# A fused attention, Mish layer and soft mixture of experts: expert weights multiplied in even-odd pairs, first expert layer handed over in halves, and a new task order

## The chip, the cores and the metric

One NeuronCore of a Trainium2 chip runs the program. Its engines are TensorE (PE: matmuls, and PEld: the weight loads that precede them), VectorE (DVE), ScalarE (ACT), GpSimd (POOL) and SyncE (SP), whose queue issues all the DMAs here. Each engine works through its own instructions in order. The metric is the device time of one execution in microseconds.

## The reference

```python
# attention, for 2 batches x 8 heads, 768 positions, 64 wide
k_sum = k.reshape(B, H, nb, 32, D).max(axis=3); v_sum = v.reshape(B, H, nb, 32, D).mean(axis=3)
scores = concat([where(|i - j| < 16, scale * q @ k.T, -1e9), scale * q @ k_sum.T + log(32)])
attn = softmax(scores) @ concat([v, v_sum])        # x: 1536 tokens x 512
h = x @ w_in                                       # 512 -> 2048
g = h * tanh(softplus(h)); x = g @ w_out           # Mish; 2048 -> 512
logits = x @ phi                                   # 8 experts x 4 slots = 32 columns
d = softmax(logits, axis=0); slot_input = d.T @ x  # 32 slot vectors of 512
slot_out[e] = relu(slot_input[e] @ w1[e]) @ w2[e]  # e = 0..7, 512 -> 1024 -> 512
out = softmax(logits, axis=1) @ slot_out
```

The layer w_out is never applied to the tokens: phi is multiplied into w_out once (W2), the logits are g @ W2, and the slot inputs are (d.T @ g) @ w_out.

## The kernel before

The 1536 tokens are 12 tiles of 128. The program first makes a list of tasks (`add`), and then emits them in the sequence of a table of task numbers, `ORDER`; a second table, `CHOICE`, says which engine takes a task that two could take. PSUM banks and SBUF slots are drawn from rings (`Ring`, `Hold`) as the tasks are emitted. So the tables fix the order on every engine, and the hardware only waits where data or a buffer is missing. In the rows below, `slot` is an SBUF slot of 8 KB for each partition and `bank` a PSUM bank; three banks (bank_61 to bank_63 in the order rows) hold the hidden layer's results.

For each tile t:

- Scores, L384 (mask) and L389; the row maximum on DVE (L400), negated on POOL or DVE (L404); exponentials on ACT (L414); normalised (L425, L426, L430); transposed on PE (L436); multiplied with the values (L446). The result goes to float16 as a high part on ACT (L451) and a low part on DVE (L452): that is x of the tile, and what the hidden layer waits for.
- Hidden layer: four blocks `fb` of 512 columns, each 12 float16 matmuls (L601, L602, L603, four times), into one bank, which ACT empties with the Mish function (L609).
- Routing: the Mish output g is split and transposed by DMA (tiles 0 to 9; L625, L627, L630) or transposed on PE (tiles 10 and 11, L642), multiplied with W2 into logits (L682, L685), summed over the four column groups (L700), turned into exponentials (L720), transposed (L734, L735), and multiplied with g (L757) into a running sum P_acc.

Ahead of that the weights w_in arrive as 64-bit words that ACT and DVE decode (L465, L467, L468), scale (L496, L289 to L297) and split (L502 high, L504 low); w_out the same way (L465 to L468, then L557 to L562 for W2, and L578 turns it). ACT has to load another function table (ACT_TABLE_LOAD) when it goes from exponentials or decodes to Mish or back.

The tail, after the last tile: P_acc is transposed (L881), multiplied with w_out (L890), scaled on DVE (L894), spread to the slot layout (L899, L905). Expert layer 1 (L921) is 64 matmuls with 32 weight columns each, so that one takes a quarter of TensorE's columns, a column group: expert e uses groups 0 and 1 when e is even, 2 and 3 when it is odd, and all go into one bank.

```python
    for k in range(16):
        e_, i = divmod(k, 2)
                    g = 2 * (e_ % 2) + half
                    pe.matmul(banks[hh.slot][32 * g:32 * g + 32], siM[:, 2 * i + c, 32 * e_:32 * e_ + 32], w[:, c, 512 * half:512 * half + 512], start=(e_ < 2 and i == 0 and c == 0), stop=(e_ >= E - 2 and i == 1 and c == 1), tile_position=(0, 32 * g))
```

Then relu (L926), transposes (L928), four copies into the layout for layer 2 (L934), and layer 2 (L975) in two stages: 384 output columns (weights w2a), then 128 (w2b). Each stage is multiplied with the token softmax, which three groups of transposes (L954) and copies (L955 to L957) prepare: L980 to L982 and L993 for the first stage, L995 for the second; L1003 and L1005 scale the results, L1007 stores them. L661 is a matmul whose result nobody reads, issued while PE would idle (18 times). The expert weights, 33.5 MB, come through L859 into slots as these come free.

Of the kernel before, what the change touches and what calls it, by code (L numbers as in the profile page):

```python
# [92 lines left out]
]  # L95
CHOICE = {
    "ACT": [
# [30 lines left out]
class Plan:  # L128
# [4 lines left out]
    def __init__(self):  # L133
        self.tasks = []
# [948 lines left out]
```

## Time and profile before

| | |
|---|---|
| device time, median of 3 runs | 315.11 us (314.45 to 315.95) |
| span of the profiled execution, first to last instruction | 314.3 us |
| busy: PE, ACT, DVE, POOL | 277.4, 202.7, 199.0, 41.5 us |
| granted TensorE clock, mean | 0.997 |
| DMA | 83.71 MB, 266 GB/s over the span |

The profiled execution's own time is its span with what lies before its first and behind its last instruction; only the span is in the profile, and the median is 0.8 us above it. Busy times of PE count matmuls that overlap as one. The granted clock is a share of 2.4 GHz.

### The profile page before, as it was taken

The numbers are of one execution on the slowest core, as the hardware profiler recorded it, in microseconds if no ns is written. First come the engines' busy times: TensorE is split into PE (matmuls) and PEld (weight loads), VectorE is DVE, ScalarE is ACT, GpSimd is POOL, SyncE is SP. The second block draws the span as 40 slices with busy tenths as digits, with TensorE's granted clock in tenths as the row PEclk, the third lists the DMA queues.
The fourth block names the chain that finished last, engine by engine and source line by source line (L and its number), as shares of the span: only waits on it lengthen the run. The fifth ranks groups of instructions, "written<-read, shape, count | busy, mean of one in ns | idle before, by whom it ended". The sixth has DMA issues, their size and how long they took to land.

```text
span 314.3 us, 7472 instructions
## 1 busy us (share of the span) xinstructions
PE 277.4 (88%) x2991; PEld 150.1 (48%) x2991; DVE 199.0 (63%) x454; ACT 202.7 (64%) x480; POOL 41.5 (13%) x54
## 2 busy tenths in 40 slices
PE   0336568789999999999999999999999999999992
PEld 0223435446555554646545445454455664334472
DVE  2589989989875877866696885774414544101271
ACT  1369889699856957887987597929647671002153
POOL 0020426403110122411101100100000010100000
PEclk9999999999999999999999999999999999999998
DMA  7999988996967487599269977898988998999948
GB/s 254 350 398 405 360 305 295 279 347 234 273 218 201 143 182 163 132 330 261 37 99 301 200 108 202 210 272 205 152 330 322 332 393 299 378 424 423 418 143 272
DMA packets 60435, 83.71 MB, mean 266 GB/s; under 512 B 44529, under 2 KB 48113, under 8 KB 56049
## 3 DMA queue, kind: packets, MB, share of 16 engines
q1 hardware_dynamic: 60400, 83.24, 85.9%
q8 instruction: 23, 0.38, 0.5%
q14 instruction: 12, 0.09, 0.1%
HBM read 69.60 MB, written 3.15 MB: 231 GB/s over the span
## 4 chain that ended last, share of the span: by engine, by line
PE 76%; DVE 9%; DMA 7%; ACT 3%; issue 3%; SPq 1%; POOL 1%; ACTq 0%; POOLq 0%; DVEq 0%
PE bank L601 13%; PE bank L602 12%; PE bank L603 12%; PE bank L921 5%; PE bank L975 5%; PE bank L757 4%; PE bank L389 4%; PE bank L446 3%; PE bank L436 3%; DMA slot<-wo 3%; PE bank L682 2%; PE bank L578 2%; DMA mask_sb<-masks 2%; DVE slot L468 2%; DMA slot<-kb 2%
## 5 line engine op out<-in xcount | busy, mean ns | idle before, releaser
L601 PE MATMUL bank<-slot,slot 128*128 128x512 f16 x192 | 73.4, 382 | 1.2 <-ACT slot L609 1.2
L602 PE MATMUL bank<-slot,slot 128*128 128x512 f16 x192 | 73.0, 380 | 0.0
L603 PE MATMUL bank<-slot,slot 128*128 128x512 f16 x192 | 72.8, 379 | 0.0
L609 ACT ACTIVATE slot<-bank,scal 128x512 f32<-128x512 f32 x48 | 32.3, 686 | 12.1 <-PE bank L603 11.6
L430 POOL TENSOR_TENSOR slot<-slot,sm 128x480 f32<-128x480 f32 x18 | 21.2, 1179 | 119.7 <-DVE sm L426 75.7
L630 DVE SCALAR_TENSOR_TENSOR slot<-slot,sc,slot 128x512 f16<-128x512 f32 x40 | 31.3, 789 | 2.4 <-ACT slot L625 2.0
L603 PEld LDWEIGHTS <-slot 128*128 128x128 f16 x192 | 18.8, 98 | 22.8 <-issue 0.3
L601 PEld LDWEIGHTS <-slot 128*128 128x128 f16 x192 | 18.8, 98 | 22.2 <-issue 5.5
L465 ACT ACTIVATE slot<-slot 128x1024 f32<-128x1024 f32 (+1 forms) x22 | 19.2, 897 | 14.4 <-DMA slot<-wi 10.7
L602 PEld LDWEIGHTS <-slot 128*128 128x128 f16 x192 | 18.8, 98 | 16.2 <-issue 1.4
L414 ACT ACTIVATE slot<-bank,sm 128x120 f32<-128x120 f32 x64 | 22.1, 363 | 3.7 <-POOL sm L404 3.7
L609 ACT ACT_TABLE_LOAD x18 | 23.1, 1283 | 0.3
L468 DVE SCALAR_TENSOR_TENSOR slot<-slot,slot 128x1024 int32<-128x1024 int32 (+1 forms) x22 | 22.5, 1025 | 0.6
L436 PE MATMUL bank<-ident_sb,slot 128*120 128x128 f32 x96 | 15.8, 289 | 6.4 <-POOL slot L430 5.5
L263 DVE COPY slot<-bank 120x512 f32<-120x512 f32 (+2 forms) x26 | 16.4, 638 | 6.0 <-PE bank L578 3.5
L261 ACT COPY slot<-bank 128x512 f32<-128x512 f32 (+1 forms) x23 | 13.1, 585 | 9.7 <-PE bank L436 5.0
L436 PEld LDWEIGHTS bank<-ident_sb,slot 128*120 128x120 f32 x96 | 11.6, 143 | 11.1 <-POOL slot L430 6.7
L627 DVE TENSOR_SCALAR slot<-slot,sc 128x512 f16<-128x512 f32 x31 | 15.7, 529 | 1.6 <-DMA slot<-slot 1.6
L446 PE MATMUL bank<-slot,slot 120*64 120x64 f32 x384 | 14.8, 233 | 1.7 <-DMA slot<-vh 1.7
L921 PE MATMUL bank<-slot,slot 128*32 128x512 f32 x128 | 15.9, 595 | 0.0
L446 PEld LDWEIGHTS bank<-slot,slot 120*64 120x64 f32 x384 | 13.1, 145 | 5.7 <-issue 2.1
L975 PE MATMUL bank<-slot,slot 128*32 128x384 f32 (+1 forms) x256 | 15.5, 381 | 0.0
(154 smaller groups left out, 460.1 us busy)
## 6 DMA issues: line engine op xcount, KB each, us to landing
slot<-w SPq DMA_DIRECT2D x16, 1024.0 KB, 7.4
slot<-w2a SPq DMA_DIRECT2D x12, 960.0 KB, 7.2
slot<-wo SPq DMA_DIRECT2D x8, 1024.0 KB, 7.4
slot<-wi SPq DMA_DIRECT2D x6, 1024.0 KB, 8.2
slot<-kh SPq DMA_DIRECT2D x12, 384.0 KB, 6.5
slot<-vh SPq DMA_DIRECT2D x12, 384.0 KB, 7.4
slot<-w2b SPq DMA_DIRECT2D x4, 1024.0 KB, 17.9
slot<-kb SPq DMA_DIRECT2D x4, 768.0 KB, 5.9
```

Source lines behind the costliest of these rows:

```text
L414: sca.activation(A_b[ha.slot][:, hp], src, AF.Exp, bias=m[:, hp:hp + 1], scale=1.0 if late else 0.125, accum_out=m[:, 4 + hp:5 + hp])
L430: (pool if e == "POOL" else vec).tensor_tensor(A_b[ha.slot], A_b[ha.slot], sm_t[hq.slot][:, 4:8].unsqueeze(2).to_broadcast([128, 4, KW]), ...
L436: pe.transpose(banks[ht.slot][0:KW, 128 * hp:128 * hp + 128], A_b[ha.slot][:, hp], ident_sb)
L446: pe.matmul(banks[hm.slot][64 * r:64 * r + 64, 128 * hp + 64 * w:128 * hp + 64 * w + 64], Vb[i][:, w, c:c + 64], AT_b[hat2[r].slot][0:KW, ...
L468: d = add("DVE", dve(n), lambda e: vec.scalar_tensor_tensor(di(), st(0), 29, di(), op0=ALU.logical_shift_right, op1=ALU.bitwise_or), [d], ...
L601: pe.matmul(ps, x[:, 0, dc], w[:, 0, dc], start=(dc == 0), stop=False)
L602: pe.matmul(ps, x[:, 0, dc], w[:, 1, dc], start=False, stop=False)
L603: pe.matmul(ps, x[:, 1, dc], w[:, 0, dc], start=False, stop=(dc == 3))
L609: d = add("ACT", act(512) + 93, lambda e, fb=fb, hb=hb, sc=sc: sca.activation(slots[gd.slot][:, 512 * fb:512 * fb + 512], banks[hb.slot], ...
L630: d = add("DVE", dve(512) + 66, lambda e: vec.scalar_tensor_tensor(pv(1), g(), sfb[:, t // TB:t // TB + 1], pv(0), op0=ALU.mult, op1=ALU.s ...
L921: pe.matmul(banks[hh.slot][32 * g:32 * g + 32], siM[:, 2 * i + c, 32 * e_:32 * e_ + 32], w[:, c, 512 * half:512 * half + 512], start=(e_ < ...
L975: pe.matmul(banks[hh.slot][32 * j:32 * j + 32, 0:nc_], hM(fc // 4)[:, j, 32 * e_:32 * e_ + 32], w[:, o:o + nc_], start=(e_ == 0 and fc < 4 ...
```

## The change

Expert layer 1 is done by pairs of experts, even and odd: of each weight half the even expert's two matmuls (groups 0 and 1) are followed at once by the odd one's (groups 2 and 3). Experts 0 to 3 go into one bank and 4 to 7 into a second, and relu, transposes and copies are done once for each. The scaling L894 and the spreading L899 and L905 are cut into two halves of the columns; layer 1 needs only the first half to begin, and layer 2 only the first four experts.

All tables are new: `ORDER`, `CHOICE` and a third one, `SLOT`, that names each buffer (ring sizes and buffers are the same). Nothing else of the arithmetic differs; the weights w1 are loaded in the order of the pairs.

```diff
-        d = add("PE", 980, l1, [d, ex_ready[k]], p + 1, acq=[hh] if k == 0 else [], use=[ex_h[k]] + ([hh] if k else []))
...
-    d = add("ACT", act(512), lambda e, hh=hh: sca.activation(hs_t, banks[hh.slot], AF.Relu), [d], p + 1, use=[hh])
...
+    for u in range(2):
+        hh, ht2 = Hold(hring), Hold(tring)
+        for pr in range(2 * u, 2 * u + 2):
+            for i in range(2):
+                def l1(e, pr=pr, i=i, hh=hh):
+                    for c in range(2):
+                        for par in range(2):
+                            w = slots[ex_h[4 * pr + 2 * i + par].slot].rearrange("p (c f) -> p c f", c=2)
+                            for half in range(2):
+                                g, e_ = 2 * par + half, 2 * pr + par
+                                pe.matmul(banks[hh.slot][32 * g:32 * g + 32], siM[:, 2 * i + c, 32 * e_:32 * e_ + 32], w[:, c, 512 * half:512 * half + 512], start=(pr % 2 == 0 and i == 0 and c == 0), stop=(pr % 2 == 1 and i == 1 and c == 1), tile_position=(0, 32 * g))
...
-            src, n = w1[k // 2, k % 2].rearrange("p c f -> p (c f)"), 2048
...
+            kind, src, n = "ld_w1", w1[2 * (k // 4) + k % 2, k // 2 % 2].rearrange("p c f -> p (c f)"), 2048
...
 ORDER = [
-    7, 11, 8, 13, 23, 29, 2, 33, 21, 34, 35, 210, 3, 36, 211, 213, 30, 31, 214, 215, 32, 37, 38, 0, 41, 42, 43, 45,
```

What the tables do to the engines is shown in three places. The first is the start, where two engines move: SP's queue, before: its rows from the load of w_in's second block (`wi`, into slot_82) to that of the first tile's values (`vh`).

```order
L476 DMA slot_82<-wi 128x2048
L270 DMA bmean_sb<-bmean 128x144
L476 DMA slot_80<-wi 128x2048
L313 DMA slot_79<-vn 128x1536
L368 DMA slot_89<-qh 128x512
L369 DMA slot_90<-kh 128x768
L476 DMA slot_81<-wi 128x2048
L476 DMA slot_82<-wi 128x2048
L368 DMA slot_88<-qh 128x512
L370 DMA slot_88<-vh 96x1024
```

The same stretch of the queue of the changed kernel:

```order
L420 DMA slot_82<-wi 128x2048
L248 DMA bmean_sb<-bmean 128x144
L285 DMA slot_79<-vn 128x1536
L420 DMA slot_80<-wi 128x2048
L328 DMA slot_89<-qh 128x512
L329 DMA slot_90<-kh 128x768
L420 DMA slot_81<-wi 128x2048
L330 DMA slot_88<-vh 96x1024
```

The values of the first tile now stand ahead of one block of w_in (1024 KB) and one `qh` (256 KB). On ACT the rows between the x of tile 1 (the high part, L451) and the first Mish (L609), before; L414 are exponentials, L465 decodes, L502 the high part of w_in.

```order
L502 ACTIVATE slot_75<-slot_83,sm_113 128x1024
L414 ACTIVATE slot_91,sm_106<-bank_65,sm_106 128x120 x4
L414 ACTIVATE slot_91,sm_108<-bank_64,sm_108 128x120 x4
L465 ACTIVATE slot_76<-slot_80 128x1024
L451 ACTIVATE slot_92<-bank_68,scal 128x512
L465 ACTIVATE slot_77<-slot_81 128x1024
L465 ACTIVATE slot_77<-slot_82 128x1024
L609 ACT_TABLE_LOAD
L609 ACTIVATE slot_85<-bank_61,scal 128x512
L502 ACTIVATE slot_74<-slot_84,sm_107 128x1024
L609 ACTIVATE slot_85<-bank_62,scal 128x512
```

After, where the same operations are L403 (x), L529 (Mish), L368, L411 and L443:

```order
L443 ACTIVATE slot_75<-slot_83,sm_107 128x1024 x2
L403 ACTIVATE slot_92<-bank_67,scal 128x512
L240 COPY slot_91<-bank_66 120x512
L411 ACTIVATE slot_76<-slot_81 128x1024
L411 ACTIVATE slot_84<-slot_82 128x1024
L368 ACTIVATE slot_91,sm_108<-bank_64,sm_108 128x120 x4
L529 ACT_TABLE_LOAD
L529 ACTIVATE slot_85<-bank_63,scal 128x512
L529 ACTIVATE slot_85<-bank_61,scal 128x512
L529 ACTIVATE slot_85<-bank_62,scal 128x512
L403 ACTIVATE slot_92<-bank_68,scal 128x512
```

The first Mish now stands behind one decode of w_out (slot_76) instead of four (slot_76 and slot_77), and the x of tile 2 right behind three of them. The second engine is PE, in mid-program, around the multiplication of tile 3's exponentials with g (L757, bank_68; L436 is a transpose of another tile's attention weights, L601 to L603 are the hidden layer), before.

```order
L601 MATMUL bank_63<-slot_73,slot_92 128x512
L602 LDWEIGHTS slot_92
L602 MATMUL bank_63<-slot_73,slot_92 128x512
L603 LDWEIGHTS slot_92
L603 MATMUL bank_63<-slot_73,slot_92 128x512
L436 MATMUL bank_64<-ident_sb,slot_91 120x128 x4
L757 MATMUL bank_68<-slot_83,en_119 32x512 x4
L601 LDWEIGHTS slot_92
```

The same multiplication after (L651), with the scores L346, the values L399 and the logits L581:

```order
L633 MATMUL bank_68<-ident_sb,lp 128x32
L346 MATMUL bank_64<-slot_90,slot_88 64x120 x2
L346 MATMUL bank_65<-slot_90,slot_88 64x120 x2
...
L651 MATMUL bank_68<-slot_83,en_119 32x512 x4
L399 MATMUL bank_67<-slot_91,slot_88 64x64 x16
L581 LDWEIGHTS slot_88
L581 MATMUL bank_62<-slot_94,slot_88 32x128
```

Groups of matmuls that use a part of TensorE's rows or columns (scores, values, logits, L757) stand next to each other now. Over the whole program, PE goes 36 times from such a group to a full-array matmul, 61 times before; into a hidden-layer matmul 10 times, 33 before; into a transpose 15 times, 20 before; into another one, such as the sum L700, 11 times, 8 before. The third place is PE at expert layer 1, its first experts before (each row is four matmuls on column groups 0 and 1 or, from slot_82 on, on 2 and 3).

```order
L661 MATMUL bank_62<-mask_sb,spread_sb 128x480
L921 MATMUL bank_63<-slot_80,slot_94 32x512 x4
L921 MATMUL bank_63<-slot_81,slot_94 32x512 x4
L921 MATMUL bank_63<-slot_82,slot_94 32x512 x4
L921 MATMUL bank_63<-slot_90,slot_94 32x512 x4
L921 MATMUL bank_63<-slot_83,slot_94 32x512 x4
```

After, its first rows and its end (L781 spreads, L811 transposes for layer 2, L836 transposes for the softmax, L855 is layer 2):

```order
L781 MATMUL bank_68<-rep_sb,vsum 128x32 x2
L803 MATMUL bank_61<-slot_80,slot_94 32x512 x2
L803 MATMUL bank_61<-slot_81,slot_94 32x512 x2
...
L803 MATMUL bank_62<-slot_85,slot_94 32x512 x2
L803 MATMUL bank_62<-slot_92,slot_94 32x512 x2
L811 MATMUL bank_66<-ident_sb,vsum 128x128 x4
L836 MATMUL bank_61<-ident_sb,P_acc 128x128 x4
L811 MATMUL bank_65<-ident_sb,gx_t 128x128 x4
L855 MATMUL bank_62<-slot_95,slot_94 32x384 x4
```

Now every two matmuls are followed by two on the other column groups, and the two groups of transposes stand behind all 128, with one of the softmax's between them. The matmuls L661 that stood between the spreading and the first weights are gone. Of the three groups of transposes for the softmax (L954, now L836) one stands ahead of layer 2 in both kernels; the second stood in the middle of the first stage of layer 2 and the third at its end, and now both stand behind it.

## Rows read from the trace of the kernel before

**Rows 1.** Busy tenths of PE in 40 slices of the span.

```profile
PE   0336568789999999999999999999999999999992
```

**Rows 2.** Windows: span, busy PE, PEld, DVE, ACT, POOL, clock, DMA share, GB/s.

```profile
0.00:45.19 45.19, 18.24 (x200) 12.26 (x200) 33.73 (x68) 28.66 (x70) 8.87 (x18) 1.00 0.98 357
45.19:63.92 18.73, 15.00 (x156) 8.44 (x153) 18.28 (x35) 15.11 (x32) 9.37 (x9) 1.00 0.88 263
63.92:261.58 197.66, 197.10 (x2148) 107.21 (x2147) 134.34 (x319) 149.40 (x359) 22.22 (x26) 1.00 0.84 227
261.58:314.30 52.72, 47.04 (x492) 22.20 (x492) 12.64 (x35) 9.53 (x23) 1.06 (x1) 0.98 0.87 338
```

**Rows 3.** Timeline of PE, start: start, duration, operation, wait before and its releaser.

```profile
36.03 1.98 PE L446 MATMUL bank<-slot,slot 120*64 120x64 f32 x32 [1.68 <-DMA slot<-vh]
...
45.19 0.61 PE L601 MATMUL bank<-slot,slot 128*128 128x512 f16 x1
...
63.92 0.38 PE L601 MATMUL bank<-slot,slot 128*128 128x512 f16 x1 [1.22 <-ACT slot L609]
```

**Rows 4.** One window of the start, columns as in the second group.

```profile
20.00:40.00 20.00, 10.75 (x124) 7.52 (x124) 18.65 (x35) 17.60 (x33) 3.73 (x4) 1.00 1.02 385
```

**Rows 5.** Timeline of DVE: low parts of x for tiles 0, 1, 2.

```profile
41.23 0.74 DVE L452 SCALAR_TENSOR_TENSOR slot<-bank,scal,slot 128x512 f16<-128x512 f32 x1
...
59.87 0.74 DVE L452 SCALAR_TENSOR_TENSOR slot<-bank,scal,slot 128x512 f16<-128x512 f32 x1
...
72.61 0.74 DVE L452 SCALAR_TENSOR_TENSOR slot<-bank,scal,slot 128x512 f16<-128x512 f32 x1
```

**Rows 6.** Timeline of ACT ahead of the first Mish.

```profile
60.69 1.19 ACT L465 ACTIVATE slot<-slot 128x1024 f32<-128x1024 f32 x1 [2.88 <-DMA slot<-wo]
61.89 1.28 ACT L609 ACT_TABLE_LOAD   x1
```

**Rows 7.** Chain of work that ended last, 170 to 198 us: start, duration, what.

```profile
170.63 0.22 PE bank L700 x2
...
173.23 0.32 PE bank L601
173.55 0.21 PE bank L602
...
174.63 0.44 PE bank L436 x4
...
195.42 0.58 PE bank L436 x4
...
197.00 0.42 PE bank L700 x2
```

**Rows 8.** Timeline of PE in the tail.

```profile
261.58 3.64 PE L890 MATMUL bank<-slot,W 128*32 128x512 f32 x32 [0.35 <-ACT W L261]
...
267.71 15.90 PE L921 MATMUL bank<-slot,slot 128*32 128x512 f32 x128
...
285.94 5.35 PE L975 MATMUL bank<-slot,slot 128*32 128x384 f32 x60
291.22 0.66 PE L954 MATMUL bank<-ident_sb,P_acc 128*128 128x128 f32 x4
291.81 6.00 PE L975 MATMUL bank<-slot,slot 128*32 128x384 f32 x68
...
300.76 0.96 PE L993 MATMUL bank<-s_split,c_split 96*128 96x384 f32 x4
```

**Rows 9.** Timeline of ACT and of DVE between the expert layers.

```profile
283.66 0.60 ACT L926 ACTIVATE vsum<-bank 128x512 f32<-128x512 f32 x1 [21.85 <-PE bank L921]
...
285.20 0.62 DVE L934 COPY slot<-bank 128x64 f32<-128x64 f32 x4 [16.82 <-PE bank L928]
```

**Rows 10.** Windows from the last hidden matmul on, columns as before.

```profile
249.60:298.60 49.00, 48.58 (x442) 21.80 (x440) 11.57 (x38) 11.56 (x26) 2.12 (x2) 1.00 0.98 390
266.00:298.00 32.00, 32.00 (x289) 12.42 (x289) 3.39 (x15) 2.73 (x5) 1.06 (x1) 1.00 1.01 411
```

More of the change, by code (lines that the diff above doesn't have):

```diff
@@ L121 @@
 class Hold:
     def __init__(self, ring):
-        self.ring, self.users, self.end, self.slot, self.home = ring, 0, 0.0, None, ring
+        self.ring, self.home, self.users, self.slot, self.n = ring, ring, 0, None, None
 class Plan:
-    LAT = PR['lat']
     def __init__(self):
-        self.tasks = []
-    def add(self, eng, dur, fn, deps=(), prio=0.0, acq=(), use=(), lat=0.0):
-        t = dict(cost=eng if isinstance(eng, dict) else {eng: dur}, fn=fn, deps=[d for d in deps if d is not None], prio=prio, acq=list(acq), use=list(acq) + list(use), end=None, lat=lat, tab=0)
+        self.tasks, self.holds = [], []
@@ L138, in add @@
+    def add(self, engines, name, fn, deps=(), acq=(), use=(), tab=0, give=None, after=()):
+        t = dict(engines=engines.split(), name=name, fn=fn, deps=[d for d in deps if d is not None], after=[d for d in after if d is not None], acq=list(acq), use=list(acq) + list(use), tab=tab, give=give, done=False)
         for h in t["use"]:
             h.users += 1
+            if h.n is None:
+                h.n = len(self.holds)
+                self.holds.append(h)
         self.tasks.append(t)
@@ L143, in run @@
     def run(self):
-        clock, table = {}, 0
-        engine = {n: e for e, ns in CHOICE.items() for n in ns}
+        choice = {n: e for e, ns in CHOICE.items() for n in ns}
         for n in ORDER:
             t = self.tasks[n]
-            e = engine.get(n) or next(iter(t["cost"]))
-            start = clock.get(e, 0.0)
-            for d in t["deps"]:
-                same = d["eng"] == e and e not in ("DMA", "none")
-                start = max(start, d["end"] + (0.0 if same else self.LAT + d["lat"]))
+            assert all(d["done"] for d in t["deps"] + t["after"])
             for h in t["acq"]:
                 if h.slot is None:
-                    free = min(h.ring.free)
-                    h.ring.free.remove(free)
-                    h.slot = free[1]
-                    start = max(start, free[0] + self.LAT)
-            t["fn"](e)
-            t["eng"], t["end"] = e, start + t["cost"][e] + (1400.0 if t["tab"] and table and t["tab"] != table else 0.0)
-            table = t["tab"] or table
-            if e != "none":
-                clock[e] = t["end"]
+                    h.slot = SLOT[h.n]
+                    h.ring.free.remove(h.slot)
+            t["fn"](choice.get(n) or t["engines"][0])
+            t["done"] = True
+            if t["give"]:
+                t["give"][0].free.update(t["give"][1])
             for h in t["use"]:
                 h.users -= 1
-                h.end = max(h.end, t["end"])
                 if h.users == 0:
-                    h.home.free.append((h.end, h.slot))
-def act(n, psum=True, ptr=0):
-    return 0.83 * n + 160 if psum else 0.7 * n + 340 + 90 * ptr
-def dve(n, fast=False, psum=False):
-    return (0.52 if fast else 1.04) * n + 70 + 55 * psum
-def dma_ns(kib):
-    return kib * 1024 * 128 / (390.0 if kib > 6.5 else 345.0)
+                    h.home.free.add(h.slot)
+        assert len(ORDER) == len(self.tasks)
 @with_exitstack
@@ L650, in g_transpose, with tr @@
-        gT_h[t, fb] = h, done
-    chain = [None]
-    pacc = [None]
-    ssum_done = [None]
+        (g,) = g_done[t, fb]
+        def tr(e):
+            for j in range(4):
+                pe.transpose(banks[ht.slot][:, 128 * j:128 * j + 128], slots[g_h[t].slot][:, 512 * fb + 128 * j:512 * fb + 128 * j + 128], ident_sb)
+        q = add("PE", ("GT", t, fb), tr, [g], acq=[ht, h], use=[g_h[t]], after=gp_hi[-1:] + [last_G[0]])
+        last_G[0] = q
+        gT_h[t, fb] = h, [add("ACT DVE", ("GTc", t, fb), lambda e: copy_on(e, gT_b[h.slot].rearrange("p a k -> p (a k)"), banks[ht.slot]), [q], use=[ht, h])]
@@ L657, in local_summary_attention_mish_soft_moe, with busy @@
+    chain, pacc, ssum_done = [None], [None], [None]
     hw = Hold(hring)
-    def busy(after, n):
-        for _ in range(n):
-            add("PE", 200, lambda e: pe.matmul(banks[hw.slot][:, 0:480].rearrange("p (a k) -> p a k", a=4), spread_sb, mask_sb[:, 0].unsqueeze(1).to_broadcast([128, 4, KW]), start=True, stop=True), [after], -50.0, acq=[hw])
+    def busy(after, n, where):
+        for j in range(n):
+            add("PE", ("busy", where, j), lambda e: pe.matmul(banks[hw.slot][:, 0:480].rearrange("p (a k) -> p a k", a=4), spread_sb, mask_sb[:, 0].unsqueeze(1).to_broadcast([128, 4, KW]), start=True, stop=True), [after], acq=[hw])
@@ L855, in local_summary_attention_mish_soft_moe @@
             n = 384 * min(5, 64 - c)
[L856 removed]
+            kind, src = "ld_w2a" if n == 1920 else "ld_w2z", w2a[:, 384 * c:384 * c + n]
         else:
[L858 to L860 removed]
+            kind, src, n = "ld_w2b", w2b[k - 29].rearrange("p e c f -> p (e c f)"), 2048
+        ex_l.append(add("DMA", (kind, k), lambda e, h=h, src=src, n=n: dma(out=slots[h.slot][:, 0:n], in_=src), acq=[h], after=ex_l[-1:]))
         ex_h.append(h)
[L862 to L867 removed]
+    ex_ready = ex_l
     siM = part(22, 0, 1152).rearrange("p (c s) -> p c s", c=4)
@@ L908, in local_summary_attention_mish_soft_moe @@
     hx = Hold(expring)
     hM = lambda half: part(hx.slot, 0, 1152).rearrange("p (c s) -> p c s", c=4) if half else siM
[L910 removed]
+    hs_b = [hs_t, gx_t]
+    d = None
+    h_ok = []
     ex_done = {}
[L912 to L925 removed]
```

479 lines of the change are left out of this document (195 added, 284 removed), and 145 rows, old and new, of tables (CHOICE, ORDER, SLOT).

## The prediction

> **What bounds the kernel now.** I read the busy tenths first [rows 1]: PE is near full from about the eighth of forty slices to the last but one, and empty only at the start. Cutting the span into four stretches [rows 2] makes this exact. Up to 45.19 us, where the hidden layer begins on PE, PE is busy 18.24 us; up to 63.92, where the first Mish lets it go on [rows 3], 15.00 of 18.73. The idle time of both is 26.95 + 3.73 = 30.68 us. From 63.92 to 261.58 PE is busy 197.10 of 197.66 us, while DVE has 134.34 and ACT 149.40: PE bounds this stretch, and time can be saved there only by issuing PE's work earlier or by making it cheaper. The tail of 52.72 us is PE again (47.04), and DMA at 338 GB/s beside it. The granted clock is 1.00 in the first three stretches and 0.98 in the last, so I let it alone. The kernel is therefore the start, plus a fixed amount of PE work, plus the tail, and I price the change in these three.
>
> **Start (-7 us).** What holds PE here is in the rows. The values of tile 0 made PE wait 1.68 us, until 36.03 [rows 3]. The low half of x ends at 41.97, 60.61 and 73.35 for tiles 0, 1 and 2 (start plus 0.74) [rows 5], and the hidden layer of a tile can't begin before that. On ACT the first Mish is behind a decode that waited 2.88 us for w_out, to 60.69, took 1.19, and is followed by a table load of 1.28 [rows 6].
>
> After, the load of the values passes one block of w_in and one qh, 1024 + 256 KB or 1.31 MB; at the 385 GB/s of 20 to 40 us [rows 4] they land 3.4 us sooner, so the values matmul starts near 32.6. Its 1.98 us, then the x halves, put x of tile 0 ready near 38.3, and the first hidden matmul near 38.5 instead of 45.19, also because the scores of the next tile no longer stand ahead of the hidden matmuls behind a wait for a bank. I estimate x of tile 1 near 55.5 (5 us sooner) and of tile 2 near 62 (11 sooner), since three decodes of w_out move behind it on ACT and the values behind fewer loads. The first Mish has one decode ahead instead of four, which frees it of the wait of 2.88; I put it near 56 and PE's going on near 58.
>
> What this is worth: at 64.4 us the changed PE has 72 hidden matmuls behind it (the blocks fb 0 to 3 of tile 0 and some of tile 1 by the order), the old one 36 at 63.92. A hidden matmul behind another costs 0.21 to 0.22 us (the second of a run of them [rows 7]), so 36 are 7.8 us. Scores (1.5) and values (1.1) of the next tiles are done sooner too, less the 0.5 by which 64.4 is later: about 9.8 us. Against this speaks that the engines feeding PE have no slack here: from 20 to 40 us DVE is busy 18.65 and ACT 17.60 of 20 us [rows 4], and DVE 18.28 of 18.73 up to 63.92 [rows 2]. What is done sooner has to be done with engines 90 to 97% full. I take 7, nearer the upper bound since nothing of the work is added, and keep 0 (the idle time only moves to another wait) and 10 as ends.
>
> **Middle (-2.2 us).** PE's work is the same in number and shape, but the order groups the matmuls that use a part of the array. The first full-array matmul after such a group takes longer: 0.32 us (after the values) where the next one takes 0.21 [rows 7]. Transposes take 0.58 instead of 0.44 for four, and the sum L700 0.42 instead of 0.22 for two [rows 7]. By the order, hidden matmuls stand behind such a group 23 times less, transposes 5 times less, sums and others 3 times more: 23 x 0.11 + 5 x 0.14 - 3 x 0.20 = 2.6; I take 2.2, as the records' ends are modelled. Bounds are 0, if the longer row hides in the pipeline, and 2.6.
>
> All other edits of the tables I cost at nothing, because PE's 99.7% leaves no room in which DVE or ACT work shows. Eleven more of the float16 splits go from DVE to ACT (at 134 and 149 of 197 us neither is full), three normalisations from POOL, six table loads less on ACT (1.28 each [rows 6], 7.7 us of ACT time, not on the path). The cover is PE's queue of ready hidden blocks; if it runs dry, the third rival applies.
>
> **Tail (-3.2 us).** The parts are these.
> - Layer 1 took 15.90 us for 128 matmuls [rows 8]. L890 has matmuls of the same shape over all four groups: 32 in 3.64 us. That is eight steps of four at 0.43 us and 0.2 besides, so 128 over all groups are 32 x 0.43 + 0.2 = 13.9 (-1.9). Before, PE got to nearly this rate in the middle of the run, as it can start the next expert's groups while the others are still busy, and lost it at both ends. Bounds: 0 (it is order alone) and -2.1.
> - From the last of L890 (265.22 by its duration) to the first weights of layer 1 at 267.71 are 2.49 us [rows 8], with scaling, 8 small matmuls and a copy in series. In halves of the columns only the first half of each is ahead: 1.5 (-1.0).
> - From the end of layer 1 (283.61) to layer 2 at 285.94 are 2.33 us [rows 8]: relu 0.60 and four copies 0.62 [rows 9], with transposes between. After, the transposes of the second half wait for its relu, but its copies are needed only by expert 4: 0.60 + 0.44 and 0.2 of hand-over, 1.25 (-1.1).
> - One group of transposes leaves the middle of the first stage, 0.59 (291.22 to 291.81) [rows 8] (-0.6).
> - Two chains of the softmax now stand behind that stage instead of one. From its end (291.81 + 6.00) to the first L993 at 300.76 are 2.95 us [rows 8]; I put the new gap at 3.8 (+0.9). And 56 instead of 40 matmuls of the second stage remain at 128 columns after the first of them (+0.5).
> The sum is -3.2; bounds -5, if the two last parts are nothing, and +1, if the first three are.
>
> **Sum.** 314.3 - 7 - 2.2 - 3.2 = 301.9 us of span. The profiled execution's span is 0.8 us below the median of the runs, 315.11, so I forecast 302.7 us.
>
> **Rivals.**
> *1. The start's idle time only moves.* ACT and DVE are in order and nearly full, so an early x of tile 0 may be paid by a late one of tile 3. For it: the windows above. Against it: two of the waits are for DMAs whose loads really move. Only middle and tail would remain: 314.3 - 5.4 + 0.8 = 309.7 us.
> *2. The weights' DMA bounds the tail.* The last hidden matmul ends where the first of two windows begins, at 249.6 [rows 10]. Eighteen weight loads were left then by the queue's issues; about 21 are in the changed order, 1 MB each or 21.4 MB, because layer 1's slots come free later. PE would need the last of them some 54 us after that matmul (15.5 of work up to L890, 3.6, 1.5, 13.9, 1.3, 11.3, then about 7). At 411 GB/s, the rate of 266 to 298 [rows 10], they take 52 us: 2 us to spare. At 390, the mean of 49 us, 55: one late. At 357, the rate of the first stretch [rows 2], 60: 6 us late, which eats more than the gain of the tail, and gives 302.7 + 6 = 308.7. The Trainium skill ("DMA: Bandwidth & Descriptors", Where 436 GB/s comes from) says of transfers between HBM and SBUF that "the HBM side (~358) binds"; by it this rival, at its 308.7, would be the case. The trace speaks against it, with 411 GB/s over 32 us of the same loads.
> *3. A new stall in the middle: slower.* PE is in order, and a block of column-group matmuls now stands together ahead of hidden matmuls that are ready. If the data of the block (exponentials from ACT, transposed by DMA) is late by more than 1 us in each of the 12 tiles, the order loses 12.4 us and the gain is gone. For it: three hidden banks leave PE only three blocks of 12 matmuls, 7.8 us, of work to go on with. Against it: between the same tasks I count about as much PE work in the new order as in the old; only two places are tight (0.65 and 1.03 us). At 1.3 us a tile the time is 318.
> *4. The pairs don't do what they say*: PE already overlaps, and layer 1 stays at 15.8: 304.6, inside the range.
>
> **How the numbers follow.** The forecast or rival 4: 0.64, with 297 to 306.5 as its own range (start -10 to -4, middle and tail by their bounds). Rival 1: 0.16. Rival 2: 0.08. Rival 3: 0.08 over 316, and 0.04 that a weaker stall ends between. The range 297 to 311 leaves out rival 3 and a little at either end. A difference of 0.5% (1.6 us) is about what measurement of this kernel can tell from none, so faster means below 313.5: 0.64 + 0.16 + 0.08 = 0.88, less 0.02 for tails; same 0.06; slower 0.08.
>
> **What would show it.** Right: the first hidden matmul near 38.5 us without a wait for vh; PE going on after the first Mish before 60; PE idle for under 1 us from there to the expert layers; layer 1 in about 14 us; the gaps at both sides of layer 1 near 1.5 and 1.25 us; no wait for a weight. Wrong: a row of the hidden layer or of the scores in the middle with waits adding to more than 3 us; x of tile 1 or 2 as late as before; layer 2's second stage waiting for w2b; layer 1 above 15.5.

## The result and the profile after

The changed kernel takes 303.95 us (median of 4 runs, 302.84 to 304.82), the kernel before 314.78 in the same set: ratio 0.9652, 95% interval 0.9614 to 0.969, faster by 10.8 us. The profiled execution's span is 303.0 us, 11.3 below that of before. Its busy times, and the windows cut at the same three events as [rows 2] (first hidden matmul, an arbitrary point behind the first Mish, first matmul of the tail), columns as there:

```profile
PE 268.8 (89%) x2995; PEld 151.4 (50%) x2995; DVE 196.3 (65%) x453; ACT 202.1 (67%) x489; POOL 30.8 (10%) x47
```

```profile
0.00:37.99 37.99, 15.21 (x199) 10.48 (x199) 28.26 (x58) 24.99 (x60) 9.16 (x20) 0.93 0.96 355
37.99:58.00 20.01, 19.18 (x203) 10.59 (x200) 19.58 (x40) 18.60 (x47) 3.97 (x5) 0.97 0.97 294
58.00:252.09 194.09, 189.48 (x2108) 108.32 (x2106) 135.71 (x318) 146.34 (x356) 16.64 (x22) 1.00 0.85 232
252.09:303.00 50.91, 44.94 (x494) 22.00 (x493) 12.76 (x40) 12.21 (x31) 1.06 (x1) 0.99 0.95 380
```

Put beside [rows 2], the 11.3 us fall into three parts:

| stretch | before: span, PE busy, idle | after | difference |
|---|---|---|---|
| start to first hidden matmul | 45.19, 18.24, 26.95 | 37.99, 15.21, 22.78 | -7.20 |
| from there to the tail | 216.39, 212.10, 4.29 | 214.10, 208.66, 5.44 | -2.29 |
| tail | 52.72, 47.04, 5.68 | 50.91, 44.94, 5.97 | -1.81 |

The cut at the first hidden matmul isn't the whole of the prediction's start, which goes on to where the first Mish lets PE continue. PE's total up to the tail doesn't depend on such a cut: its idle time falls from 31.24 to 28.22 us, by 3.0, and its busy time from 230.34 to 223.87, by 6.5.

PE in the start (timeline as in [rows 3]) and the low halves of x on DVE, which answer to [rows 5]:

```profile
28.09 1.05 PE L346 MATMUL bank<-slot,slot 64*64 64x120 f32 x32
...
32.44 1.92 PE L399 MATMUL bank<-slot,slot 120*64 120x64 f32 x32
...
36.18 1.88 PE L346 MATMUL bank<-slot,slot 64*64 64x120 f32 x32 [0.90 <-DMA slot<-kh]
37.99 0.61 PE L523 MATMUL bank<-slot,slot 128*128 128x512 f16 x1
...
62.92 0.38 PE L525 MATMUL bank<-slot,slot 128*128 128x512 f16 x1
```

```profile
35.97 0.72 DVE L404 SCALAR_TENSOR_TENSOR slot<-bank,scal,slot 128x512 f16<-128x512 f32 x1
54.56 0.75 DVE L404 SCALAR_TENSOR_TENSOR slot<-bank,scal,slot 128x512 f16<-128x512 f32 x1
62.74 0.75 DVE L404 SCALAR_TENSOR_TENSOR slot<-bank,scal,slot 128x512 f16<-128x512 f32 x1
```

The values of tile 0 start at 32.44 and wait for no transfer. x of tiles 0, 1 and 2 is ready at 36.69, 55.31 and 63.49. The row at 62.92 is the 72nd hidden matmul, where before the 36th was done by 63.92. The scores of the old start are slower than the row at 28.09; one of its three rows is

```profile
28.75 1.88 PE L389 MATMUL bank<-slot,slot 64*64 64x120 f32 x32
```

PE in the tail, to be read against [rows 8]:

```profile
252.09 4.01 PE L759 MATMUL bank<-slot,W 128*32 128x512 f32 x32
...
257.68 13.94 PE L803 MATMUL bank<-slot,slot 128*32 128x512 f32 x128
...
273.01 10.12 PE L855 MATMUL bank<-slot,slot 128*32 128x384 f32 x120
283.51 0.85 PE L855 MATMUL bank<-slot,slot 128*32 128x384 f32 x8 [0.38 <-DMA slot<-w2a]
...
288.75 0.44 PE L873 MATMUL bank<-s_split,c_split 96*128 96x384 f32 x1 [0.61 <-ACT slot L839]
```

Layer 1 takes 13.94 us instead of 15.90. Layer 2 starts 1.39 us behind its end (271.62 to 273.01) instead of 2.33, and once, for 0.38 us, waits for a weight.

### The profile page after: what moved, and what is told of

Read it like the earlier page. It is cut to its first block, busy times and chain, and to the rows that moved or that the text cites. A ratio compares the mean times of both kernels' runs of the same rounds, so it can differ in the third digit from the quotient of the medians.

```text
span 303.0 us, 7485 instructions
## 1 busy us (share of the span) xinstructions
PE 268.8 (89%) x2995; PEld 151.4 (50%) x2995; DVE 196.3 (65%) x453; ACT 202.1 (67%) x489; POOL 30.8 (10%) x47
## 4 chain that ended last, share of the span: by engine, by line
PE 46%; DVE 20%; DMA 19%; ACT 9%; issue 3%; SPq 1%; DVEq 0%; POOL 0%; ACTq 0%
PE bank L523 7%; PE bank L524 7%; PE bank L525 7%; DMA slot<-w2a 6%; DMA slot<-wo 5%; ACT slot L368 3%; DVE slot L413 3%; DVE slot L444 3%; PE bank L651 2%; PE bank L506 2%; DMA slot<-kb 2%; PE bank L803 2%; DMA gx_t<-slot 2%; DVE slot L412 2%; DMA slot<-vn 2%
## 5 line engine op out<-in xcount | busy, mean ns | idle before, releaser
L523 PE MATMUL bank<-slot,slot 128*128 128x512 f16 x192 | 73.2, 381 | 0.0
L525 PE MATMUL bank<-slot,slot 128*128 128x512 f16 x192 | 73.0, 380 | 0.0
L529 ACT ACTIVATE slot<-bank,scal 128x512 f32<-128x512 f32 x48 | 31.7, 685 | 17.9 <-PE bank L525 16.6
L242 DVE COPY slot<-bank 120x512 f32<-120x512 f32 (+4 forms) x33 | 17.8, 555 | 37.1 <-ACT gx_t L810 13.6
L525 PEld LDWEIGHTS <-slot 128*128 128x128 f16 x192 | 18.8, 98 | 23.1 <-issue 0.6
L523 PEld LDWEIGHTS <-slot 128*128 128x128 f16 x192 | 18.9, 98 | 19.6 <-issue 1.9
L411 ACT ACTIVATE slot<-slot 128x1024 f32<-128x1024 f32 (+1 forms) x22 | 19.3, 888 | 13.4 <-DMA slot<-wi 9.9
L383 POOL TENSOR_TENSOR slot<-slot,sm 128x480 f32<-128x480 f32 x15 | 17.3, 1158 | 91.5 <-DVE sm L379 54.5
L368 ACT ACTIVATE slot<-bank,sm 128x120 f32<-128x120 f32 x64 | 22.1, 363 | 1.1 <-POOL sm L358 0.7
L413 DVE SCALAR_TENSOR_TENSOR slot<-slot,slot 128x1024 int32<-128x1024 int32 (+1 forms) x22 | 20.5, 937 | 0.4
L240 ACT COPY slot<-bank 128x512 f32<-128x512 f32 (+4 forms) x26 | 13.2, 525 | 10.1 <-PE bank L506 6.1
L412 DVE TENSOR_SCALAR slot<-slot 128x1024 int32<-128x1024 int32 (+1 forms) x22 | 13.4, 614 | 8.6 <-ACT slot L411 8.5
L346 PE MATMUL bank<-slot,slot 64*64 64x120 f32 x384 | 14.3, 292 | 3.0 <-DMA slot<-kh 3.0
L341 PE MATMUL bank<-mask_sb,spread_sb 128*64 128x480 bf16 (+1 forms) x24 | 5.7, 430 | 12.4 <-DMA mask_sb<-masks 11.2
L346 PEld LDWEIGHTS bank<-slot,slot 64*64 64x64 f32 x384 | 11.3, 147 | 8.6 <-issue 8.3
L855 PE MATMUL bank<-slot,slot 128*32 128x384 f32 (+1 forms) x256 | 15.1, 381 | 0.4 <-DMA slot<-w2a 0.4
L399 PEld LDWEIGHTS bank<-slot,slot 120*64 120x64 f32 x384 | 12.9, 144 | 4.7 <-issue 2.3
```

Of the source, the lines that this page charges most:

```text
L242: vec.tensor_copy(dst, src)
L346: pe.matmul(banks[hs2[r].slot][64 * w:64 * w + 64, KW * hp:KW * hp + KW], Qb[i][d, 4 * w + hp], Kb[i][d, :, 4 * w + hp], start=late, stop= ...
L368: sca.activation(A_b[ha.slot][:, hp], src, AF.Exp, bias=m[:, hp:hp + 1], scale=1.0 if late else 0.125, accum_out=m[:, 4 + hp:5 + hp])
L383: (pool if e == "POOL" else vec).tensor_tensor(A_b[ha.slot], A_b[ha.slot], sm_t[hq.slot][:, 4:8].unsqueeze(2).to_broadcast([128, 4, KW]), ...
L411: d = add("ACT", ("dec_a%d" % n,) + name, lambda e: sca.activation(dst(), st(1).bitcast(F32), AF.Prelu, scale=2.0 ** -112, alpha=-(2.0 ** ...
L412: d = add("DVE", ("dec_s%d" % n,) + name, lambda e: vec.tensor_scalar(di(), di(), 3, None, op0=ALU.logical_shift_left), [d], use=use)
```

## The experiments

The theory is the sum of the prediction, three stretches that add. The rival is that the start's gain hangs on the order behind it, and by itself only moves idle time (the prediction's first rival). Each set ran beside the kernel before on one chip, so the runs of different sets are compared by their ratios to it. The changed kernel was run once more for this, unaltered.

> The changed kernel once more, unaltered, as the measure for the other runs of this set: 304 to 304.7 us, 0.965 of the kernel before. Both theories say the same; the spread of its runs says what the others can tell.

It took 304.17 us (303.9 to 305.91), ratio 0.9647 (0.9602 to 0.9692). Differences of about 1 us between the runs that follow say little.

### The start

**One load put back** (the rows of SP's queue):

```diff
 L420 DMA slot_81<-wi 128x2048
-L330 DMA slot_88<-vh 96x1024
 L420 DMA slot_82<-wi 128x2048
 L328 DMA slot_88<-qh 128x512
+L330 DMA slot_88<-vh 96x1024
 L329 DMA slot_90<-kh 128x768
```

> The changed kernel with one load moved on SP's queue: the first tile's values again behind one block of w_in and one qh, 1.31 MB. Theory (the load's place is what made the start earlier): the values matmul waits for vh until some 35.8 us instead of starting at 32.4, the first hidden matmul comes near 40.5 instead of 38, and the time is 2 to 3 us longer, 306.5. Rival (ACT and DVE order the start, and PE has slack to take it up): below 1 us, 304.5.

It took 306.28 us (305.14 to 309.56), 2.1 us more than the unaltered kernel in the same set (303.9 to 305.91, so the spreads touch). Its PE timeline:

```profile
35.59 1.98 PE L414 MATMUL bank<-slot,slot 120*64 120x64 f32 x32 [3.61 <-DMA slot<-vh]
...
40.22 0.61 PE L538 MATMUL bank<-slot,slot 128*128 128x512 f16 x1
```

The wait for vh is back, to 35.59 us, the first hidden matmul comes 2.2 us later than in the rows above, and by the medians the whole kernel is later by as much, as expected.

The traces say less. These are the windows from the first hidden matmul to the tail, in this run, in the changed kernel, and in the changed kernel's second trace:

```profile
40.22:252.16 211.94, 208.76 (x2308) 118.90 (x2304) 154.90 (x357) 165.10 (x405) 20.36 (x26) 1.00 0.85 238
37.99:252.09 214.10, 208.66 (x2309) 118.91 (x2305) 155.29 (x357) 164.94 (x402) 20.61 (x27) 1.00 0.86 238
36.45:251.31 214.86, 208.04 (x2308) 118.66 (x2304) 156.13 (x358) 165.75 (x405) 21.41 (x28) 1.00 0.85 239
```

The sooner the hidden layer begins, the longer PE idles behind: 3.18, 5.44 and 6.82 us. Of the 3.77 us between the first and the last of these starts, 0.85 are left at the tail. In these three executions most of a lead has moved into later waits, in the changed order too. That the medians keep 2.1 us where the traces keep less stays open.

**The same load moved forward in the kernel before**, the mirror image (rows of SP's queue again):

```diff
+L370 DMA slot_88<-vh 96x1024
 L476 DMA slot_82<-wi 128x2048
 L368 DMA slot_88<-qh 128x512
-L370 DMA slot_88<-vh 96x1024
```

> The kernel before with one load moved on SP's queue: the first tile's values ahead of one block of w_in and one qh, where the changed kernel has them; all else as before. If the load's place alone makes the earlier start, the first hidden matmul comes near 42 instead of 45.2 us and the time is 2 to 3 us shorter, 313. Theory after the spliced kernels (an earlier start is lost behind the old order, since DVE and ACT set its pace up to 80 us): below 1 us, 315.

It took 316.54 us (314.29 to 318.48), ratio 1.0029 (1.0003 to 1.0054): no gain, if anything a loss. Its PE and ACT timelines say why:

```profile
35.24 0.45 PE L451 MATMUL bank<-slot,slot 120*64 120x64 f32 x2 [0.39 <-DMA slot<-vh]
...
39.23 1.97 PE L451 MATMUL bank<-slot,slot 120*64 120x64 f32 x30 [3.54 <-ACT slot L266]
...
47.03 0.39 PE L606 MATMUL bank<-slot,slot 128*128 128x512 f16 x1
```

```profile
33.49 1.14 ACT L470 ACTIVATE slot<-slot 128x1024 f32<-128x1024 f32 x1 [1.00 <-DMA slot<-wi]
...
37.44 1.12 ACT L470 ACTIVATE slot<-slot 128x1024 f32<-128x1024 f32 x1 [1.77 <-DMA slot<-wi]
38.59 0.59 ACT L266 COPY slot<-bank 120x512 f32<-120x512 f32 x1
```

The values come 0.8 us sooner (35.24 against 36.03), but w_in lands later, and ACT decodes w_in (L470) ahead of the copy (L266) that the same multiplication needs. PE does two of its 32 matmuls and waits 3.54 us for that copy. In the changed order ACT's copies stand ahead of those decodes, so the load's new place is worth something only with ACT's new order.

**Spliced orders.** These are three kernels with the changed kernel's code, in which the order of tasks is cut, and engines and buffers go with the order. In outline (not lines of the kernels):

```text
tail_only = old order ahead of the tail + changed tail
start     = changed order up to its 72nd hidden task + what is left, in the order of tail_only
middle    = old order up to its 36th hidden task + what is left, in the changed order
```

A hidden task is three matmuls (L523 to L525), so these cuts come later than the names, and the expectations, say: at the 216th hidden matmul of the changed order and at the 108th of the old one. In the traces PE's matmuls follow the changed kernel up to 118.2 us in `start`, and `tail_only` up to 85.6 us in `middle`.

> The changed kernel's code, with the order, engines and buffers of the kernel before for everything ahead of the tail, and the changed tail behind it. If the two traces' stretches add (tail 52.72 us before, 50.91 after), the tail alone gives 1.8 us: 313.0 us. By the forecast's own tail term, 3.2 us, it would be 311.6. The rival that the order ahead of the tail makes all of the difference, as the tail waits for weights, says 314.8.

It took 315.1 us (312.98 to 318.26), ratio 0.9962 (0.993 to 0.9993): the tail alone gives about 1.2 us, with an interval that nearly reaches none. In its trace the tail is 50.43 us, 2.3 shorter than before, and what is ahead of it 1.1 us longer.

> The changed order up to its 72nd hidden matmul, then the order of before for all that is left, then the changed tail. Theory (the start's idle time is worth its full length to a PE that is full behind it): 313.0 less the 7.2 us by which the first hidden matmul is earlier, 305.8 us. Rival (the idle time only moves to a later wait): 312 to 313.

It took 314.41 us, ratio 0.9961 (0.9924 to 0.9997), and not 305.8. Beside the tail, the changed order up to 118 us gives nothing when the old order follows it.

> The spliced kernel with the changed start and the order of before behind it, again, for a trace: its runs gave 314.4 us where the sum of the stretches said 305.8. If the start's gain is lost by waits further on (rival 1 of the prediction), the first hidden matmul stands near 38 us as in the changed kernel, and PE is idle for some 7 to 9 us more between there and the tail than before, in waits for DVE or ACT work or for transfers. If the splice itself spoils the start, the first hidden matmul is late.

This run took 314.04 us. Its window from the first hidden matmul to the tail, then from the cut of the order to the tail, and from the same matmul on in the changed kernel:

```profile
37.27:261.67 224.40, 217.08 (x2313) 117.14 (x2309) 159.39 (x367) 167.09 (x400) 23.83 (x29) 0.99 0.85 234
118.18:261.67 143.49, 140.33 (x1456) 74.92 (x1454) 89.18 (x234) 99.77 (x241) 11.35 (x12) 0.99 0.83 218
118.10:252.09 133.99, 132.51 (x1451) 76.89 (x1451) 84.90 (x223) 97.11 (x242) 7.59 (x9) 1.00 0.85 222
```

The hidden layer begins as early as in the changed kernel, and at 118 us PE is still level with it. What is lost is lost behind: for the same work, a few matmuls that nobody reads aside, the old order takes 143.49 us from there to the tail and the changed one 133.99. Of these 9.5 us, 1.7 are idle time and 7.8 busy time. I had expected 7 to 9 us more of idle time than before, and it is 3.0 (7.32 against 4.29). Part of the busy time is the clock, behind two waits:

```profile
126.80 0.65 PE L404 MATMUL bank<-ident_sb,slot 128*120 128x128 f32 x4 [0.93 <-POOL slot L398]
...
128.78 0.29 PE L647 MATMUL bank<-ident_sb,eT 32*128 32x32 f32 x1 [1.33 <-ACT lp L635]
...
129.11 0.61 PE L538 MATMUL bank<-slot,slot 128*128 128x512 f16 x1
129.51 0.64 PE L539 MATMUL bank<-slot,slot 128*128 128x512 f16 x1
```

Seven hidden matmuls stand about 0.43 us from the next here instead of 0.22, which makes some 1.5 us. I can't place the other 6 us of busy time. The run doesn't say what the start is worth by itself, since the cut lies far behind the start.

> The order of before up to its 36th hidden matmul, then the changed order for the rest and the changed tail. Theory (the middle gains 2.3 us by itself, whatever the start): 310.7 us, PE's first hidden matmul near 45 us as before. Rival (the middle's order is worth nothing behind the old start, or was made for the new one and stalls): 313 or more.

It took 331.1 us, ratio 1.0465 (1.0422 to 1.0508). PE at its worst place:

```profile
86.17 1.05 PE L361 MATMUL bank<-slot,slot 64*64 64x120 f32 x32
92.84 1.11 PE L404 MATMUL bank<-ident_sb,slot 128*120 128x128 f32 x4 [5.62 <-DVE slot L398]
93.75 0.63 PE L538 MATMUL bank<-slot,slot 128*128 128x512 f16 x1
94.17 0.63 PE L539 MATMUL bank<-slot,slot 128*128 128x512 f16 x1
```

PE waits 5.62 us for a normalisation on DVE, and then its hidden matmuls stand 0.42 us apart instead of 0.22, at half the clock. This wait begins 1.6 us behind the cut at 85.6 us. I take it that at a cut tasks which one order had done early and the other late come in a burst; that isn't shown. The times of the two splices are no prices of a start or a middle. They show that neither part of the changed order, cut off there, gives anything without the other.

**The clock in the start.** In the changed kernel PE does nothing from 30 to 32 us. These are windows of its start (the column ahead of the last two is the granted clock):

```profile
30.00:32.00 2.00, 0.00 (x0) 0.00 (x0) 2.00 (x4) 1.98 (x3) 1.81 (x2) 1.00 0.97 289
32.00:34.00 2.00, 1.98 (x32) 1.86 (x34) 1.83 (x11) 1.68 (x9) 0.83 (x2) 0.63 1.00 393
34.00:36.00 2.00, 1.27 (x10) 0.30 (x6) 1.97 (x5) 2.00 (x3) 0.07 (x1) 0.50 1.06 430
38.00:40.00 2.00, 2.00 (x11) 0.80 (x8) 2.00 (x2) 1.88 (x8) 0.21 (x1) 0.66 1.06 236
```

The clock falls to 1.2 GHz just as the values of tile 0 come. Fillers, matmuls that nobody reads, against that (the last two lines show only the changed call):

```diff
+    def warm(n):
+        for _ in range(n):
+            pe.matmul(banks[2][:, 0:480].rearrange("p (a k) -> p a k", a=4), spread_sb, mask_sb[:, 0].unsqueeze(1).to_broadcast([128, 4, KW]), start=True, stop=True)
...
+            warm(8 if t == 2 else 0)
             for hp in range(4):
...
-lambda e: pe.matmul(banks[hb.slot][:, 0:128], t(10).to_broadcast([128, 128]), ident_sb, start=True, stop=True)
+lambda e: [warm(11 if n == 1 else 0), pe.matmul(banks[hb.slot][:, 0:128], t(10).to_broadcast([128, 128]), ident_sb, start=True, stop=True)]
```

> The changed kernel with 19 matmuls nobody reads put where PE idles in the start (11 ahead of the scale at 32 us, 8 between the mask and the scores of tile 2), so that PE is busy from 29 us on. In the changed kernel's trace the values of tile 0 took 1.92 us and the scores of tile 2 1.88, against 1.15 and 1.05 later, with a granted clock of 0.50 from about 33 to 39 us. Theory (the half clock delays the first hidden matmuls): clock 1.00 throughout, first hidden matmul near 37.2, its first twelve in 2.6 us instead of 3.3, time 1 to 1.5 us shorter, 303. Rival (DVE sets the pace there, x and the attention weights come when they come): 304.2, no change.

It took 302.63 us (302.06 to 303.3), ratio 0.9582 (0.9544 to 0.9621): 1.5 us below the unaltered kernel of the same set, whose fastest run is above its slowest. This is the best version here. Its PE timeline:

```profile
32.64 1.15 PE L404 MATMUL bank<-slot,slot 120*64 120x64 f32 x32 [0.69 <-DMA slot<-vh]
...
36.56 1.05 PE L351 MATMUL bank<-slot,slot 64*64 64x120 f32 x32 [0.64 <-DMA slot<-kh]
37.54 0.39 PE L528 MATMUL bank<-slot,slot 128*128 128x512 f16 x1
```

Values and scores take 1.15 and 1.05 us instead of 1.92 and 1.88, and the mean clock of its six runs is 0.998 to 1.000 (0.980 to 0.993 unaltered). The size fits the theory. How it comes about is not shown: the first hidden matmul stands at 37.54, 0.45 us earlier than in the first trace of the changed kernel but 1.1 later than in the second one (36.45), in which the clock was back a little sooner. Yet its tail begins at 250.79, ahead of both (252.09 and 251.31).

### The middle

For this, 144 matmuls with zero weights, which add nothing to the result, are put into the hidden blocks, once over all columns and once over a quarter (`w_` stands for 128 or 32 here; the second has `tile_position=(0, 0)` too):

```diff
                     pe.matmul(ps, x[:, 1, dc], w[:, 0, dc], start=False, stop=(dc == 3))
+                    if dc < 3:
+                        pe.matmul(ps[0:w_, 0:128], zero[:, 0:w_], w[:, 0, dc, 0:128], start=False, stop=False)
```

> The changed kernel with 144 small matmuls more in the middle of the hidden layer's blocks (three in each of 48), with zero weights, 128 columns of output and all 128 weight columns, so that no switch between tile shapes is added. By the row of a hidden matmul, 0.216 us for 512 columns, one costs 0.05 to 0.06 us: 7 to 9 us in all, 312 us. It is the measure for the next run.

It took 308.39 us, 4 us above the changed kernel's 304.5 (0.9647 of the set's 315.66): less than I expected. From its first hidden matmul to the tail:

```profile
38.38:256.59 218.21, 216.26 (x2453) 126.89 (x2449) 154.33 (x357) 164.67 (x396) 21.91 (x26) 1.00 0.85 235
```

PE is busy 7.6 us more there than in the changed kernel (208.66), as expected, but idle only 1.95 us instead of 5.44. About half of the added work has taken the place of waits.

> The same with 32 weight columns in place of 128, on the first column group: 144 switches to a quarter of the array and back. Theory (a switch costs what the first hidden matmul behind such a group shows, 0.1 us): 14 us above the run with full columns, 326 us. If the changed order's 3.4 us less of busy time in the middle came from its 23 switches fewer, it is 0.15 each, 22 us above, 334. Rival (the longer row hides in the pipeline): within 3 us of the run with full columns.

It took 335.72 us (334.84 to 336.1). The two differ by 27.3 us, 0.19 us for a switch to a quarter of the array and back. These are rows of PE in the first, then in the second:

```profile
100.47 0.38 PE L527 MATMUL bank<-slot,slot 128*128 128x512 f16 x1
100.68 0.22 PE L529 MATMUL bank<-slot,zero 128*128 128x128 f16 x1
100.74 0.38 PE L525 MATMUL bank<-slot,slot 128*128 128x512 f16 x1
```

```profile
102.46 0.38 PE L527 MATMUL bank<-slot,slot 128*128 128x512 f16 x1
102.77 0.23 PE L529 MATMUL bank<-slot,zero 128*32 128x128 f16 x1
102.94 0.39 PE L525 MATMUL bank<-slot,slot 128*128 128x512 f16 x1
```

From one hidden matmul to the next it is 0.27 us with the small one between at full width and 0.48 with the narrow one: 0.21 for the round trip, of which 0.10 lies ahead of the narrow one (0.31 after 0.21) and 0.11 behind it (0.17 after 0.06). The rival, that the longer row hides in the pipeline, is out. The row that I priced the switch by [rows 7] shows only the way back. Other tile shapes than this one were not tried.

### The tail

**Layer 1 by expert again**, in the two banks and with the halves:

```diff
-                    for c in range(2):
-                        for par in range(2):
-                            w = slots[ex_h[4 * pr + 2 * i + par].slot].rearrange("p (c f) -> p c f", c=2)
+                    par = i
+                    for ii in range(2):
+                        w = slots[ex_h[4 * pr + 2 * ii + par].slot].rearrange("p (c f) -> p c f", c=2)
+                        for c in range(2):
...
```

> The changed kernel with only the order of layer 1's 128 matmuls put back: the eight of an even expert (groups 0 and 1), then the eight of its odd partner (groups 2 and 3); two banks and halves stay. Theory (the pairs are worth what the row shows): layer 1 takes 15.9 us instead of 13.94, and the time is 305.9 us. Rival (PE overlaps them anyway, and the shorter layer 1 came from the two banks or from the weights' arrival): 13.9 us and 304.0.

Its row in the timeline:

```profile
258.60 15.90 PE L804 MATMUL bank<-slot,slot 128*32 128x512 f32 x128
```

15.90 us, to the hundredth what it was before: the 1.96 us are due to the order of the matmuls. The time, 305.59 us (304.59 to 307.43), ratio 0.967 (0.9627 to 0.9712), can't be told from the unaltered kernel's, though it lies on the right side of it; in this run layer 2 no longer waits for its weights, which may give 0.4 back.

**One hand-over**:

```diff
-        hh, ht2 = Hold(hring), Hold(tring)
+        hh, ht2 = Hold(hring) if u == 0 else hh, Hold(tring)
...
-                    lo, hi = 4 * u + par, 4 * u + 4
+                    lo, hi = par, E
...
-[d, ex_ready[k]] + (h_ok if e_ >= 4 else h_ok[:2])
+[d, ex_ready[k]] + h_ok
```

Relu, transposes and copies of the first half are empty in it.

> The changed kernel with layer 1's result in one bank, one relu, one set of transposes and copies behind all 128 matmuls, and layer 2 waiting for all of them; the pairs stay. Theory (the halves shorten the hand-over): from the end of layer 1 to layer 2 2.3 us as before instead of 1.4, and 305.1 us. Rival (the weights of layer 2 are late anyway, by 0.4 us in the changed kernel, so that an earlier start of it is given back): 304.2 to 304.6.

```profile
256.25 13.94 PE L818 MATMUL bank<-slot,slot 128*32 128x512 f32 x128
...
272.20 3.11 PE L872 MATMUL bank<-slot,slot 128*32 128x384 f32 x36 [0.63 <-DVE slot L257]
```

From the end of layer 1 (270.19) to layer 2 are 2.01 us instead of 1.39, so the halves are worth 0.6 us in that gap. Whether the kernel keeps them stays open: 305.13 us (303.29 to 305.75), ratio 0.9667 (0.9641 to 0.9694), overlaps with the unaltered kernel, and layer 2 didn't wait for weights here either.

## Why the prediction was right, and where not

The forecast of 302.7 us is 1.25 below the 303.95 measured, within its own range. Its sum of the span was -12.4, against -11.3. Up to the tail it was -9.2 against -9.5, but with another make-up: it had 7 us of idle time gained in the start and 2.2 of busy time saved, and the traces show 3.0 of idle and 6.5 of busy time. That the two errors cancel is luck.

**Start, -7: -7.2, with two steps wrong.** The single steps came as forecast: the values at 32.44 us (32.6), the first hidden matmul at 37.99 (38.5), x of tile 1 at 55.31 (55.5), x of tile 2 at 63.49 (62), PE going on with the 37th hidden matmul at 55.36 (58), 72 hidden matmuls where the old order had 36. One reason given for it was wrong: scores still stand ahead of the first hidden matmul (36.18). And of the 7.2 us only 4.2 are idle time. Of the other 3.0, 0.6 are a pair of matmuls of the scaling (L297, now L273) that now comes behind the first hidden matmul, and some 2.4 are the same work done at a higher clock: the scores at 28.09 take 1.05 us, and all scores of the old start took 1.88. I had let the clock alone because the profile showed 1.00 there. That is the first wrong step.

The second is that PE bounds what follows, so that a lead of PE is kept. The sign for it was PE idle for under 1 us from where it goes on to the expert layers. It is idle for 4.61 us there (55.36 to 252.09), against 0.56 before (63.92 to 261.58). Across the three traces of the changed order a start 3.77 us sooner brought 3.64 us more of idle time behind. So rival 1, which I gave 0.16, is in part what happens, though its time of 309.7 us didn't come. One link of it is shown by the early vh in the kernel before: the copy behind the decodes on ACT. The whole chain is not.

**Middle, -2.2: -2.3.** This is -3.4 of busy time and +1.2 of idle, from the first hidden matmul on. The term was under-sized: a round trip between tile shapes costs 0.19 us by the difference of two runs, not the 0.11 that I read from one side of it; 23 round trips fewer are then up to 4.4, if all shapes cost like the one tried. In return waits for DVE, ACT and DMA, none over 0.95 us, took back a part. Rival 3 came, but small: its block-by-block stalls would have decided at 12.4 us. Which part of the 3.4 is switches and which is clock I can't separate.

**Tail, -3.2: -1.8.** The terms were, forecast and measured: layer 1 -1.9 and -1.96; ahead of it -1.0 and -0.91 (256.10 to 257.68); behind it -1.1 and -0.94; first stage of layer 2 -0.6 and -0.52, the wait of 0.38 included; from its end to the first L873 +0.9 and +1.44 (284.36 to 288.75); the rest +0.5 and +0.71 (288.75 to 303.00). L759 took 0.37 us more than L890 had, which I hadn't priced. The two mis-sized terms are the softmax chains behind the first stage, where the first L873 waits 0.61 for ACT, and the rest. Rival 4 is refuted by the run by expert: 15.90 against 13.94 for layer 1. In the time of the whole kernel the pairs and the halves don't show clear of the spread.

**Rival 2**, that the weights' DMA bounds the tail, is just at its edge. After the last hidden matmul the loads run at this rate:

```profile
237.40:286.40 49.00, 48.62 (x494) 23.73 (x492) 15.65 (x56) 14.12 (x39) 2.12 (x2) 1.00 1.00 408
```

408 GB/s over 49 us, between the 411 that I counted on and the 390 that would have cost a microsecond, and one wait of 0.38 us. The Trainium skill's limit of about 358 GB/s, a core's half of the 716 GB/s of a memory stack ("DMA: Bandwidth & Descriptors", Where 436 GB/s comes from), isn't the bound of this run either.

## What to carry to other kernels

A lead that one engine gets at the start is worth its length only if the engines that feed it keep up behind. Here moving the load alone gave nothing, putting it back cost 2 us by the medians, and in the traces a sooner start was mostly paid by later waits. So price the start and what follows as one, and ask of a load moved forward which load goes back and what stands in line behind that one. When a forecast adds up terms, check idle and busy time apart: a right sum can be two errors. When an order is cut for an experiment, check in the trace where the cut came to lie. Where TensorE takes tiles of different shapes in turn, count the switches: 0.19 us for a round trip here, so group them. And when matmuls fill parts of the array, issue them in turn over all column groups: 2 of 16 us of that layer for the order alone.

## What the hardware showed that I had not expected

- After 2.5 us without a matmul (29.56 to 32.02) in the changed kernel the granted clock fell to 0.50, which is 1.2 GHz, and stayed there into the first hidden matmuls; the same after 5.6 us of idle in a spliced kernel, where each hidden matmul then stood 0.42 us from the next. These gaps were thus paid twice. In the other spliced kernel waits of 0.93 and 1.33 us within 3 us came before such a stretch. 19 matmuls that nobody reads, put into the start's gaps, gave 1.5 us.
- The granted clock in the profile isn't all: in the start of the kernel before it shows 1.00 throughout [rows 2], while scores took 1.88 us there, as they do at 0.50 in the changed kernel (36.18). The durations are the better witness.
- A full-width matmul over 128 columns between two hidden ones adds 0.06 us in the timeline, but 144 of them only 4 us to the kernel, half of that: PE idled 3.5 us less between the first hidden matmul and the tail (1.95 against 5.44).
